# Cosine attention and a gated layer on one core: half products for h of chunk 2 and half of chunk 1, one order from chunk 0's last output tiles on, output stores on SyncE

## The chip, the cores and the metric

The kernel runs on 1 core of one Trainium2 chip. The metric is the device time of one execution in microseconds (us); less is better. A run of the kernel before gives 273.4 us as the median of 3 (273.35, 273.4, 274.11).

## The reference

Inputs q, k, v have the shape 8 batches x 8 heads x 576 rows x 64. w_in is 512 x 2048, w_out 2048 x 512, beta has 2048 entries. Everything is float32 in memory.

```python
theta = np.pi / 2.0 * pos / S
def phi(x, c, s):
    r = np.maximum(x, 0.0)
    return np.concatenate([r * c, r * s], axis=-1)
q_p = phi(q, cos_w, sin_w); k_p = phi(k, cos_w, sin_w)
kv  = np.einsum('bhsf,bhsd->bhfd', k_p, v); z = np.sum(k_p, axis=2)
num = np.einsum('bhsf,bhfd->bhsd', q_p, kv)
den = np.einsum('bhsf,bhf->bhs', q_p, z)[..., None] + 1e-06
x   = (num / den).transpose(0, 2, 1, 3).reshape(B * S, H * D)   # 4608 x 512
h   = x @ w_in
g   = h * (1.0 / (1.0 + np.exp(-beta * h)))
out = g @ w_out                                                # 4608 x 512
```

## The kernel before, in words

**Two halves in one stream.** The attention goes by batch b = 0 to 7, the layer by chunk c = 0 to 8 of 512 rows of x (TCH). A batch has nine blocks of 64 rows, a chunk eight, so chunk c needs the last c blocks of batch c−1 and the first 8−c of batch c. While the layer works on chunk c, the attention of batch b = c+1 is made beside it, and the raw inputs of later batches are loaded.

**Attention of one batch.** load_raw (L79) loads q, k and v of a batch by one DMA each, all issued on SyncE; there is one buffer for each of the three (raw_q, raw_k, raw_v), so the load of the next batch can start only when the last reader of the old one is done. q_relu and k_relu (L192 on ACT, L193 on DVE) take the positive part in bf16. v_scale (L217 on ACT, L219 on DVE) multiplies v by the cosine or the sine of its row; one instruction does one of nine blocks. kv_mm (L276) makes k_p^T v in PSUM and kv_take (L286) copies it out. q is transposed by one DMA, q_turn_dma (L259), on SyncE; the sine copy of it is a multiplication by tan (tan_mul, L223) on GpSimd or DVE. num_mm (L297) makes numerator and denominator, x_rden (L308, L312) the reciprocal, x_mul (L319) the quotient, and x_turn_dma (L367), again a DMA on SyncE, transposes it into xt, the chunk's input. For the first blocks of a run PE transposes instead (x_turn_pe, L356, with copies at L361 and L363).

**The layer's first product, two forms.** In the whole form (h_group) one 128-column tile of h is four matmuls of 128x512 (h_mm, L386) and one silu on ACT (h_act, L394). In the half form (h_pair) two column tiles together form a 2 by 2 block product over halves of the columns, of the depth and of the rows, done with seven products in place of eight by sums of operands (Strassen and Winograd); each product is two matmuls of 128x256 (L511). That needs four sums of w_in for each pair (wh_sum, L443, in the buffers wx["w"] and wx["v"]), four sums of x for each chunk (x_sum, L455), and in PSUM a seed copy (op "c", ACT, L480), a kept partial (op "d" ACT or "D" DVE, L484) and two additions (ops "e", "f", DVE, L487); the two silu are ops "A" and "B" (h_silu, L420). Before, chunks 0, 1 and 2 use the whole form and chunks 3 to 8 the half form.

**The second product.** Chunk 0 is whole (o_mm, L544). Chunk 1 (o_fast, L563) and chunks 2 to 8 (o_pair, L621) use the same seven products for four output tiles of 128 rows, with sums of g (g_sum, L406, into S1 to S4) and of w_out (T1 to T4, L876 to L879). Each output tile is copied to o_sb (in o_pair: A, B on ACT and X, Y on DVE, both L658/L661 as whole tiles; pieces P, Q on ACT and U, V on DVE, L652) and stored in two halves of rows (store, L537). The stores of chunks 0 to 6 are issued on GpSimd, those of chunk 7 on SyncE, those of chunk 8 on GpSimd, SyncE and ACT.

**What sets the order.** The tile framework is told to keep the program's order (manual_schedule), and each engine runs its instructions in that order. Up to chunk 1 the order is written as loops over slots: 32 slots of chunk 0 (slots 0 to 15 tiles of h, 16 to 23 and 24 to 31 the output), then 16 slots of h of chunk 1 with the attention's steps hung on some of them, then a list of o_fast's ops. Chunk 2 starts with 16 slots of whole h tiles (h_first). From chunk 2's output on, ORDERS holds a string of ops for each chunk, and chunk() runs them one after the other: "h25" is product 5 of h pair 2, "h2c5" its seed into bank 5, "ox6" product 6 of the first output pair, "s30" a sum of g, "W61" a sum of w_in, "t1" a sum of x, "K05"/"kT" kv products and copy, "N12" numerators into bank 2, "x1" the quotient and its transpose, "v3"/"w3" a v_scale of the sine on ACT / of the cosine on DVE, "k2" and "q1" relus, "g0" a multiplication on GpSimd, "TQ" the batch's q transpose, "Lq", "Lk", "Lv" a raw load. PSUM has eight banks, all named by hand; o_sb has four buffers, xt three, g five.

Of the kernel before, what the change touches and what calls it, by code (L numbers as in the profile page):

```python
# [16 lines left out]
P = 128  # L17
# [5 lines left out]
def kernel(  # L23
# [175 lines left out]
    def k_relu(b, j0=0, j1=4, eng="dve", n0=0, n1=NQ):  # L199
        relu(rk.rearrange("q n j d -> q j n d")[:, j0:j1, n0:n1], raw_tile(b, "k")[:, j0:j1, n0:n1], eng)  # L200
# [207 lines left out]
    def g_sums(c, i0, i1):  # L408
        for kind in (1, 3, 2, 4):
            got = g_sum(c, i0, i1, kind)  # L410
        return got
# [10 lines left out]
    def wx_tiles():  # L422

        wx["w"] = stage.tile([P, 4, 512], FP32, name="w_stage", tag="w_stage").rearrange("q a f -> q (a f)").bitcast(
            BF16).rearrange("q (k s g f) -> q k s g f", k=4, s=4, g=2)
        wx["v"] = stage.tile([P, 4, 512], FP32, name="w_stage", tag="w_stage").rearrange("q a f -> q (a f)").bitcast(
            BF16).rearrange("q (k s g f) -> q k s g f", k=4, s=4, g=2)
        wx["x"] = stage.tile([P, 4, 512], FP32, name="w_stage", tag="w_stage").rearrange("q a f -> q (a f)").bitcast(
            BF16).rearrange("q (s n c) -> q s n c", s=8, n=NB // 2)
        wx["q"] = stage.tile([P, 4, 512], FP32, name="w_stage", tag="w_stage").rearrange("q a f -> q (a f)").bitcast(  # L430
            BF16)[:, 0 : 2 * NQ * P].rearrange("q (s n c) -> q s n c", s=2, n=NQ)

    def w_sum(jt, i):
        return wx["w" if jt % 4 == 0 else "v"][:, jt // 4, i]

    def wh_sum(jt, kind):
        f0 = jt % 4
        A11, A12, A21, A22 = (win[jt // 4][:, 2 * jp : 2 * jp + 2, f * P : (f + 1) * P]
                              for f in (f0, f0 + 1) for jp in range(2))
        s1, s2, s3, s4 = (w_sum(jt, i) for i in range(4))  # L440
        o, l, r, op = {1: (s1, A21, A22, ALU.add), 2: (s2, s1, A11, ALU.subtract),
                       3: (s3, A11, A21, ALU.subtract), 4: (s4, A12, s2, ALU.subtract)}[kind]
        return nc.vector.tensor_tensor(o, l, r, op=op)  # L443

    def wh_sums(jt):
        for kind in (1, 3, 2, 4):
            got = wh_sum(jt, kind)
        return got
# [55 lines left out]
    def h_pair(c, i):  # L504
# [16 lines left out]
        s1, s2, s3, s4 = (w_sum(jt0, k_) for k_ in range(4))  # L521
# [10 lines left out]
    def store(c, tt, o_sb, m0=0, m1=DM, eng=None):  # L532
        for hf in range(2):
            bb, n = divmod((c * TCH + tt * P) // HP + hf, NQ)
            own = (nc.gpsimd if c < 7 or (c == NTC - 1 and tt == 0) else
                   (nc.sync, nc.scalar)[hf] if c == NTC - 1 and tt % 2 else nc.sync)
            (eng or own).dma_start(out=out_v[bb, n][:, m0:m1], in_=o_sb[hf * HP : (hf + 1) * HP, m0:m1])  # L537
# [225 lines left out]
    def rest():  # L763
# [16 lines left out]
        k_relu(1, 0, 2)  # L780
        q_relu(1, 0)
# [9 lines left out]
    def second():  # L791
# [22 lines left out]
        28: lambda: x_turn_pe(1, 0, 7, 4, ("act",), (0,)),  # L814
        29: lambda: x_turn_pe(1, 0, 7, 5, ("dve",), (1,)),
    }

    def num_rest():
        for n in range(7, NQ):
            for jp in range(2):  # L820
                num_mm(1, n, jp, 2, 2 * (n - 7) + jp)
        x_mul(x_rden(2, 0, 7, NQ, (0, 1)), 7, NQ)
        x_turn_dma(1, 7, NQ)

    def att_q(b, turn=True):
        q_relu(b, 0)
        q_relu(b, 1)
        if turn:
            q_turn_dma(b)
        if b + 1 < B and b != 3:  # L830
            load_raw(b + 1, "q")

    def v_half(b, cs, n0=0, n1=NQ, eng="dve"):
        if b >= B:
            return
        v_scale(b, cs, n0=n0, n1=n1, eng=eng)
        if cs == 1 and n1 == NQ and b + 1 < B:
            load_raw(b + 1, "v")

    def k_all(b):  # L840
        k_relu(b)
        if b + 1 < B:
            load_raw(b + 1, "k")

    def kv_all(b, bank=6, eng="dve"):
        kv_mm(b, 0, bank)
        kv_mm(b, 1, bank)
        kv_take((0, 1), bank, eng)
# [5 lines left out]
    for slot in range(32):  # L854
# [26 lines left out]
    wx_tiles()  # L881
    for slot in range(16):
        h_group(1, slot)
        if slot == 0:
            num_rest()
            att_q(2)
            v_half(2, 0)
        if 2 <= slot < 6:
            v_half(2, 1, slot + 3, slot + 4, "act")
        if slot == 4:  # L890
            k_all(2)
            v_half(2, 1, 0, 5)
        elif slot == 6:
            w_sums()
        elif slot == 10:
            kv_all(2, eng="act")
            for jp in range(2):
                tan_mul(nc.vector, qs_of(2)[:, jp], qts[0][:, jp], 0, NQ)
    q_relu(3, 0, "act")
    q_relu(3, 1, "act")  # L900
    q_turn_dma(3)

    def one_sums(kind):
        for i0 in range(0, JT // 2, 2):
            g_sum(1, i0, i0 + 2, kind)

    def ops(of, names):
        for n in names.split():
            of[n]()

    x, y = o_fast(1, 0, (2, 5, 4)), o_fast(1, 1, (3, 7, 6))
    ops(x, "1 c1")
    one_sums(1)
    ops(y, "1 c1")
    for t, bank in enumerate((4, 6, 0)):
        num_all(2, t, bank)
    one_sums(2)
    x_part(2, 0, 4)
    ops(x, "6 cu")
    ops(y, "6 cu")  # L920
    one_sums(3)
    ops(x, "2 5 c5")
    x_part(2, 1, 6)
    ops(x, "7")
    one_sums(4)
    ops(x, "a2 a7")
    ops(y, "7 2")
    got = wh_sums(0)
    x_part(2, 2, 0)
    load_raw(4, "q")  # L930
    q_tan(3, 0, got)
    q_tan(3, 1)
    ops(y, "a2 5 c5")
    ops(x, "3 a3 4 c4")
    ops(y, "a7 3 a3 4 c4")
    v_half(3, 0)

    ORDERS = {
# [153 lines left out]
```

## Time and profile before

| what | value |
|---|---|
| device time, median of 3 runs | 273.4 us (273.35 to 274.11) |
| span of the profiled execution | 272.7 us |
| time of the profiled execution beyond its span | not given; the median is 0.7 us above the span |
| granted clock of PE, 40 slices | 9 or more tenths in each |
| silu of half form (L420) / of whole form (L394) | 96 x 702 ns / 48 x 688 ns |
| additions of h (L487, first form) | 74 x 428 ns |
| seeds (L480) | 62 x 383 ns |
| sums of g (L406) | 66 x 418 ns |
| v_scale on ACT (L217) | 58 x 503 ns |
| output stores issued on GpSimd | 58, 33.9 us of issue |
| raw loads, median time from issue to landing | v 9.7, k 9.5, q 7.4 us |

How to read it: the profiler records every instruction of every engine. PE is the matmul engine, PEld its weight loads, DVE, ACT and POOL the vector, scalar and GpSimd engines, SP is SyncE, SPq its DMA issues. The busy share of an engine is the time in which it has at least one instruction running. Because instructions on one engine overlap at their ends, the mean duration of an instruction is more than the time between two of them in a stream; the latter is read from rows of the timeline, where a run of equal instructions has one start and one length.

### The profile page before, as it was taken

To read this page: it belongs to the slowest core of one execution; us is meant where nothing else is said; L and a number is where in the kernel's file an instruction comes from. 1 tells how busy PE (TensorE), PEld (TensorE's weight loads), DVE (VectorE), ACT (ScalarE), POOL (GpSimd) and SP (SyncE) were. 2 spreads that over 40 slices of the span, in tenths; PEclk is the share of its full clock that TensorE was granted. 3 is DMA by queue.
4 is the path that set the end of the run, shared out by engine and by line. 5 is a ranking of instruction groups with operands and counts; after the bars stand their busy time and mean duration, and the time that the engine had idled before them with its cause. 6 is when DMAs were issued, how large, how long until landed. Compare 5 with 4: busy or idle time off the path is not lost.

```text
span 272.7 us, 8970 instructions
## 1 busy us (share of the span) xinstructions
PE 265.3 (97%) x3712; PEld 206.8 (76%) x3712; DVE 224.0 (82%) x596; ACT 188.4 (69%) x384; POOL 68.3 (25%) x89
## 2 busy tenths in 40 slices
PE   8899999999899999999999999999999999999994
PEld 8554455455784588888888888888888888888883
DVE  5989969499989889789989997899589768757852
ACT  4778777796419656899489966996696179428920
POOL 1444000510078000660085009300840060000001
PEclk9999999999999999999999999999999999999999
DMA  6999999999969999994589439943600570015005
GB/s 237 374 395 383 392 390 319 379 201 336 284 130 311 240 348 226 240 313 103 147 216 370 92 58 223 332 71 62 181 2 2 61 185 1 2 27 130 0 2 155
DMA packets 50681, 54.00 MB, mean 198 GB/s; under 512 B 31232, under 2 KB 31760, under 8 KB 50640
## 3 DMA queue, kind: packets, MB, share of 16 engines
q1 hardware_dynamic: 47504, 45.55, 59.1%
q0 software_dynamic: 2784, 7.61, 9.6%
q8 instruction: 29, 0.48, 0.7%
q10 hardware_dynamic: 352, 0.27, 0.4%
q14 instruction: 12, 0.10, 0.1%
HBM read 36.71 MB, written 9.44 MB: 169 GB/s over the span
## 4 chain that ended last, share of the span: by engine, by line
PE 85%; DVE 9%; DMA 3%; SPq 1%; issue 1%; ACT 1%; DVEq 0%
PE ps L621 32%; PE ps L511 27%; PE ps L386 10%; PE ps L544 5%; PE ps L563 4%; PE ps L297 3%; DMA raw_v<-in_v_dram 3%; PE ps L276 3%; DVE vb L219 1%; DVE xs L319 1%; DVE qs L223 1%; SPq L79 1%; DVE S L406 1%; DVE rk L193 1%; DVE qb L193 0%
## 5 line engine op out<-in xcount | busy, mean ns | idle before, releaser
L537 POOL DMA_DIRECT2D out_dram<-o_sb x58 | 33.9, 591 | 147.3 <-ACT o_sb L658 86.3
L420 ACT ACTIVATE g_t<-ps,beta 128x512 bf16<-128x512 f32 x96 | 60.3, 702 | 1.4 <-PE ps L511 1.3
L621 PEld LDWEIGHTS <-S 128*128 128x128 bf16 x448 | 43.4, 98 | 5.2
L511 PE MATMUL ps<-w_stage 128*128 128x256 bf16 x288 | 46.6, 272 | 0.1
L386 PE MATMUL ps<-xt,win 128*128 128x512 bf16 (+1 forms) x196 | 42.8, 375 | 0.1
L511 PEld LDWEIGHTS <-w_stage 128*128 128x128 bf16 x384 | 37.3, 98 | 5.1 <-issue 0.2
L487 DVE TENSOR_TENSOR ps<-ps,p 128x256 f32<-128x256 f32 x74 | 30.5, 428 | 8.6 <-PE ps L511 3.0
L394 ACT ACTIVATE g_t<-ps,beta 128x512 bf16<-128x512 f32 x48 | 32.3, 688 | 7.2 <-PE ps L386 7.1
L621 PEld LDWEIGHTS <-g_t 128*128 128x128 bf16 x336 | 32.3, 98 | 4.5 <-ACT g_t L420 0.4
L386 PEld LDWEIGHTS <-win 128*128 128x128 bf16 x196 | 18.7, 98 | 21.1 <-issue 0.5
L511 PE MATMUL ps<-xt,win 128*128 128x256 bf16 x192 | 32.9, 273 | 0.0
L511 PEld LDWEIGHTS <-win 128*128 128x128 bf16 x288 | 28.0, 98 | 3.4
L621 PE MATMUL ps<-wout,g_t 128*128 128x256 bf16 x224 | 28.9, 273 | 0.0
L406 DVE TENSOR_TENSOR S<-g_t 128x512 bf16<-128x512 bf16 (+1 forms) x66 | 25.7, 418 | 3.3 <-ACT g_t L420 1.7
L480 ACT COPY ps<-ps 128x256 f32<-128x256 f32 x62 | 22.6, 383 | 7.5 <-PE ps L621 4.0
L217 ACT ACTIVATE vb<-raw_v,sin 128x256 bf16<-128x256 f32 (+1 forms) x58 | 26.0, 503 | 1.5 <-DMA raw_v<-in_v_dram 1.5
L621 PE MATMUL ps<-T,S 128*128 128x256 bf16 x224 | 26.6, 273 | 0.0
L621 PE MATMUL ps<-wout,S 128*128 128x256 bf16 x224 | 26.4, 273 | 0.0
L319 DVE TENSOR_TENSOR xs<-ps,rden 128x768 bf16<-128x768 f32 (+4 forms) x26 | 22.8, 884 | 0.9 <-DVE rden L312 0.2
L223 POOL TENSOR_TENSOR qs<-qt,tanr 128x1152 bf16<-128x1152 bf16 x6 | 14.3, 2387 | 27.4 <-PE ps L563 21.0
L658 ACT COPY o_sb<-ps 128x512 f32<-128x512 f32 x11 | 6.3, 587 | 20.1 <-PE ps L621 20.1
L487 DVE TENSOR_TENSOR ps<-ps,u 128x256 f32<-128x256 f32 x36 | 15.3, 427 | 5.3 <-PE ps L511 3.3
(112 smaller groups left out, 414.7 us busy)
## 6 DMA issues: line engine op xcount, KB each, us to landing
raw_v<-in_v_dram SPq DMA_DIRECT2D x7, 1152.0 KB, 9.7
raw_k<-in_k_dram SPq DMA_DIRECT2D x7, 1152.0 KB, 9.5
raw_q<-in_q_dram SPq DMA_DIRECT2D x7, 1152.0 KB, 7.4
out_dram<-o_sb POOLq DMA_DIRECT2D x58, 128.0 KB, 4.5
w_stage<-in_moe_w_in_dram SPq DMA_DIRECT2D x3, 1024.0 KB, 12.8
w_stage<-in_moe_w_out_dram SPq DMA_DIRECT2D x2, 1024.0 KB, 7.9
w_stage<-in_moe_w_out_dram SPq DMA_DIRECT2D x4, 512.0 KB, 11.9
out_dram<-o_sb SPq DMA_DIRECT2D x10, 128.0 KB, 2.4
```

Source lines behind the costliest of these rows:

```text
L217: got = nc.scalar.activation(o, a, AF.Copy, scale=t[:, n : n + 1])
L223: return eng.tensor_tensor(dst.rearrange("q n (g p) -> q n g p", g=2), src.rearrange("q n (g p) -> q n g p", g=2), tanr[:, n0:n1].unsqueez ...
L319: nc.vector.tensor_tensor(o.rearrange("q j n s d -> q j (n s) d"), nv[:, :, a:z, :, 0:D].rearrange("q j n s d -> q j (n s) d"), rden[:, :, ...
L386: nc.tensor.matmul(ps[:, h_bank(c, jt), i * 64 : (i + w) * 64], lhsT=win[jt // 4][:, mi, (jt % 4) * P : (jt % 4 + 1) * P], rhs=xt[:, i : i ...
L394: return nc.scalar.activation(gs[c, jt // 4][:, jt % 4], ps[:, h_bank(c, jt)], AF.Silu, scale=beta[:, jt : jt + 1])
L406: return nc.vector.tensor_tensor(o, l, r, op=op)
L420: return nc.scalar.activation(gs[c, jt // 4][:, jt % 4], bank, AF.Silu, scale=beta[:, jt : jt + 1])
L480: return nc.scalar.copy(at("a", 0), at("b", 0))
L487: nc.vector.tensor_tensor(dst, at("b", 0), st["p5"], op=ALU.add)
L511: nc.tensor.matmul(dst, lhsT=l[:, g], rhs=r[:, :, g * HP : (g + 1) * HP], start=start and g == 0, stop=g == 1, skip_group_check=True)
L537: (eng or own).dma_start(out=out_v[bb, n][:, m0:m1], in_=o_sb[hf * HP : (hf + 1) * HP, m0:m1])
L621: nc.tensor.matmul(dst, lhsT=l(i), rhs=r[:, i], start=start and i == 0, stop=i == order[-1], skip_group_check=True)
```

## The change

- **h of chunk 2 and of pairs 4 to 7 of chunk 1** goes to the half form. Chunk 1's first eight tiles (0 to 7) stay whole (ops "G0" to "G7").
- **Sums of w_in** are made a slice (512 columns) at a time, both pairs of it together: 16 instructions of 128x512 in place of 32 of 128x256. Six of them stand in rest(), which runs in chunk 0, the others in the new orders.
- **One order.** The slot loop ends at slot 26. The rest of chunk 0 (its last output tiles as ops "Sb" to "Sf", the last transposes on PE as "R0", "R1"), chunk 1 and all of chunk 2 become strings in ORDERS. An op may name another chunk ("1/ox6") or another batch ("r0@2"), so ops of one chunk stand among those of the next. The strings of chunks 3 to 8 are new as well: the last output ops and some sums of a chunk stand among the h ops of the next.
- **New ops**: k_relu on DVE ("l", "kk"), q_relu on ACT ("r"), a v_scale of the cosine on ACT ("z") or of the sine on DVE ("u"), the sums of w_out one by one ("M1" to "M4").
- **Stores** of chunks 0 to 7 are issued on SyncE, and of chunk 8 the first tile's on GpSimd and the others' as before.
- **Order on SyncE** around chunk 1: before, q, v, k of batch 2, a transpose of x, the q transpose of batch 2, q, k, v of batch 3, the q transpose of batch 3. After: q, v, k of batch 2, q of batch 3, the q transpose of batch 2, eight stores of chunk 0, a transpose of x, v of batch 3, k of batch 3, a transpose of x, q of batch 4.
- **The last output ops** of chunk 8: before "oyU oyf ox4 oxY oy4 oy3 oyB oyV", after "oy3 ox3 oxf oyf oxX ox4 oy4 oyU oyV oxY oyY".

The core of the diff:

```diff
-    def w_sum(jt, i):
-        return wx["w" if jt % 4 == 0 else "v"][:, jt // 4, i]
-    def wh_sum(jt, kind):
-        f0 = jt % 4
-        A11, A12, A21, A22 = (win[jt // 4][:, 2 * jp : 2 * jp + 2, f * P : (f + 1) * P]
-                              for f in (f0, f0 + 1) for jp in range(2))
+    def w_sum(sl, i):
+        return wx["wv"[sl // 2]][:, sl % 2, i]
+    def wh_sum(sl, kind):
+        A11, A12, A21, A22 = (
+            win[sl][:, 2 * jp : 2 * jp + 2].rearrange("q g (u r f) -> q g u r f", u=2, r=2)[:, :, :, r]
+            for r in range(2) for jp in range(2))
...
-        s1, s2, s3, s4 = (w_sum(jt0, k_) for k_ in range(4))
+        s1, s2, s3, s4 = (w_sum(jt0 // 4, k_)[:, :, jt0 % 4 // 2] for k_ in range(4))
...
-            own = (nc.gpsimd if c < 7 or (c == NTC - 1 and tt == 0) else
-                   (nc.sync, nc.scalar)[hf] if c == NTC - 1 and tt % 2 else nc.sync)
+            own = (nc.sync if c < NTC - 1 else nc.gpsimd if tt == 0 else (nc.sync, nc.scalar)[hf] if tt % 2 else nc.sync)
...
         k_relu(1, 0, 2)
+        wx_tiles("wv")
+        for sl, kind in ((0, 1), (0, 3), (0, 2), (0, 4), (1, 1), (1, 3)):
+            wh_sum(sl, kind)
         q_relu(1, 0)
...
-    for slot in range(32):
+    for slot in range(27):
...
+        0: (
+            "Sb R0 Sc Sd 1/M1 W21 t1 Se W31 W22 1/r1@2"),
+        1: (
+            "h417 r0@2 0/R1 0/W33 Lq@3 h45 TQ@2 0/Sf M4 G6 G7 u8@2 0/t2 h4d h4c2 u5@2 u6@2 Z0 G0 v2@2 G3 h514 h5c3 h616 "
...
+            "h72 h5f s11 h6f h76 h7e h5A kk@2 h43 Lv@3 h4B y0 h63 h54 h5B h6A h4A h64 h73 h77 G1 h7f G2 h7A y1 Lk@3 K02 "
+            "K1 h74 kT s10 h6B oy17 M2 N03 N25 h7B oyc0 x0 s20 r1@3 s13 s12 r0@3 s32 s33 v2 z3 ox12 oy2 N13 s40 oy5 ox5 "
+            "s22 s21 s23 v7 oy6 z0 v8 oxc1 oxd z7 Lq@4 z4 x1 ox2 s30 oyd z2 v3 u4 oye"),
...
+        elif k_ in "vwuz":
+            got = v_scale(batch(1), "wzvu".index(k_) // 2, n0=n, n1=n + 1, eng="act" if k_ in "vz" else "dve")
...
+    wx_tiles("xq")
+    held = None
+    for c in range(NTC):
         for op in ORDERS[c].split():
...
+            other, slash, rest_ = op.partition("/")
+            held = do(int(other), rest_, held) if slash else do(c, op, held)
```

More of the change, by code (lines that the diff above doesn't have):

```diff
@@ L420, in h_silu, with wx_tiles @@
         return nc.scalar.activation(gs[c, jt // 4][:, jt % 4], bank, AF.Silu, scale=beta[:, jt : jt + 1])
[L422 to L431, printed above, removed]
[L433 to L440 removed]
+    def wx_tiles(names):
+        for name in names:
+            t = stage.tile([P, 4, 512], FP32, name="w_stage", tag="w_stage").rearrange("q a f -> q (a f)").bitcast(BF16)
+            if name in "wv":
+                wx[name] = t.rearrange("q (k s g u f) -> q k s g u f", k=2, s=4, g=2, u=2)
+            elif name == "x":
+                wx[name] = t.rearrange("q (s n c) -> q s n c", s=8, n=NB // 2)
+            else:
+                wx[name] = t[:, 0 : 2 * NQ * P].rearrange("q (s n c) -> q s n c", s=2, n=NQ)
+    def w_sum(sl, i):
[4 more added lines that the diff above has]
+            for r in range(2) for jp in range(2))
+        s1, s2, s3, s4 = (w_sum(sl, i) for i in range(4))
         o, l, r, op = {1: (s1, A21, A22, ALU.add), 2: (s2, s1, A11, ALU.subtract),
@@ L899 @@
[L899 to L919, printed above, removed]
@@ L1058, with w_out_sum, pair @@
-    h_first(2)
-    held = None
-    for c in range(2, NTC):
-        held = chunk(c, held)
+    def w_out_sum(kind):
+        z = ALU.subtract
+        o, l, r = {1: (T1, B12, B11), 2: (T2, B22, T1), 3: (T4, B21, T2), 4: (T3, B22, B12)}[kind]
+        return nc.vector.tensor_tensor(o, l, r, op=z)
+    ORDERS = {
[70 rows of a table added]
+    }
+    pairs, parts = {}, {}
+    def pair(c, name):
+        if (c, name) not in pairs:
+            n = "xy".find(name[1])
+            pairs[c, name] = (h_pair(c, int(name[1])) if name[0] == "h" else o_pair(c, n) if name[0] == "o" else
+                              o_fast(c, n, ((2, 5, 4), (3, 7, 6))[n]))
+        return pairs[c, name]
```

196 lines of the change are left out of this document (64 added, 132 removed), and 100 rows, old and new, of the table ORDERS.

## The prediction

> **What bounds the kernel now.** I read the busy times first, then the chain of work that ended last, then the order in time of each engine.
>
> ```profile
> span 272.7 us, 8970 instructions
> PE 265.3 (97%) x3712; PEld 206.8 (76%) x3712; DVE 224.0 (82%) x596; ACT 188.4 (69%) x384; POOL 68.3 (25%) x89
> ...
> PE 85%; DVE 9%; DMA 3%; SPq 1%; issue 1%; ACT 1%; DVEq 0%
> ```
>
> PE is busy 97% of the span and carries 85% of the chain, and the granted clock is at its top in all forty slices. So time falls only if PE gets less to do or stops less. In the timeline of PE, from 18.65 us to its last end at 269.02, one idle stretch is longer than 0.25 us: 0.96 us ahead of chunk 1's output products.
>
> ```profile
> 51.70 8.81 PE L386 MATMUL ps<-xt,win 128*128 128x512 bf16 x40
> 61.59 4.49 PE L386 MATMUL ps<-xt,win 128*128 128x512 bf16 x20
> 70.15 1.91 PE L563 MATMUL ps<-T,S 128*128 128x256 bf16 x16 [0.96 <-ACT p L602]
> 104.31 1.04 PE L621 MATMUL ps<-wout,g_t 128*128 128x256 bf16 x8
> 105.18 1.91 PE L621 MATMUL ps<-wout,S 128*128 128x256 bf16 x16
> ```
>
> Columns: start, length, engine, line, operation, shape, count. These rows give what a matmul costs in a stream, which isn't the mean duration of the group table (375 and 273 ns there, because matmuls overlap). Twenty more of 128x512 take 8.81 − 4.49 us: **0.216 us each**. Eight more of 128x256 take 1.91 − 1.04: **0.109 us each**.
>
> **The products (fewer, smaller matmuls).** Twelve pairs of h tiles (eight in chunk 2, four in chunk 1) leave the whole form, 2 tiles x 4 matmuls of 128x512 = 8 per pair, for seven products of two 128x256 = 14 per pair. 96 x 0.216 = 20.7 us go, 168 x 0.109 = 18.3 us come: **−2.4 us** of PE. [...]
>
> **The work around the products.** Each half-product pair brings a seed (ACT, L480), a keep, two adds (DVE, L487) and two silu; each sum of w_in and of x is made once. Counted from the two orders, adds go 124 to 152, seeds 62 to 76, x sums 24 to 32, and the 32 small w_in sums become 16 of twice the width. With their mean durations this is about +8 us on DVE and +16 on ACT over the whole kernel. Neither can bound it on average (224 and 188 of 272), but locally it can: from the rest of batch 1's numerators to chunk 2's kv products I count, at the pace that these engines keep back to back (length less 0.08 us on DVE, less 0.11 on ACT), 24.5 us of DVE (62 instructions) and 24.1 of ACT (52) beside 25.2 of PE, and in the first 11 us DVE has 12.1 to PE's 11.0. The later stages, whose orders before are as full, lose about 0.1 us in 10. I take **+0.3 us**; the bounds are 0 and 62 x 0.08 = 5.0 us, the latter if no two DVE instructions overlapped their ends, which the rows of before (1.42 us for four of 0.416) exclude. The range takes +1.1, DVE's excess over those 11 us. The six w_in sums in chunk 0 (not shown by the trace in this shape; between 0.28, the small form, and 0.42, the x sum of the same size) are 6 x 0.34 = 2.0 us, in 2.25 us that DVE idles there from 36.9 us, waiting for raw_q: nothing. With that cover gone it would be 2.0 on DVE, still ahead of PE's need. Moving stores off GpSimd saves nothing by itself: its 58 issues (33.9 us) delay only GpSimd's own multiplications, which nothing here waits for.
>
> **The stall at 69 us.** The chain in order of time ends its DVE stretch with sums for chunk 1's output:
>
> ```profile
> 66.66 2.02 DVE S L406 x6
> 68.69 1.15 ACT qb L192
> 69.83 0.27 ACT p L602
> 70.15 4.86 PE ps L563 x43
> ```
>
> ACT's q relu of batch 3 stands in front of the copy that PE waits for. In the new order half of chunk 1's h work lies between those sums and their readers, and the relus stand after them; this stall goes: **−1.0 us** (bounds 0, if DVE is late there again, and −1.0). Late next are batch 3's v rows, below.
>
> **SyncE.** Batch transposes and raw loads are issued there, in order:
>
> ```profile
> 61.46 0.39 SPq L79 DMA_DIRECT2D raw_v<-in_v_dram  x1
> ...
> 69.86 3.51 SPq L259 DMA_TRANSPOSE qt<-qb  x1
> ...
> 110.12 1.50 SPq L79 DMA_DIRECT2D raw_q<-in_q_dram  x1
> 111.73 11.25 SPq L259 DMA_TRANSPOSE qt<-qb  x1
> ...
> 139.62 0.46 SPq L79 DMA_DIRECT2D raw_q<-in_q_dram  x1
> 140.18 10.77 SPq L259 DMA_TRANSPOSE qt<-qb  x1
> ...
> 266.31 3.82 SPq L537 DMA_DIRECT2D out_dram<-o_sb  x6
> ```
>
> A transpose of q holds the queue 3.5 to 11.3 us. Each time the hold ends when the loads issued ahead of it have landed: that raw_q lands 12.8 us after its issue, at 122.92, and the hold ends at 122.98; the next lands at 150.97, the hold ends at 150.95. The change puts q of batch 3 in front of batch 2's transpose, and behind that the eight stores of chunk 0 (0.636 us each, 3.82 / 6), a transpose of x and only then v and k of batch 3. Walking the queue: v and k of batch 2 land at 52.3 and 55.2 us, as before (40.83 + 11.5, 41.43 + 13.8); q of batch 3, issued at about 50, lands 2.9 behind them (their spacing), at 58.2; until then the transpose holds SyncE. Stores to 63.3, the x transpose (1.25) to 64.6, v of batch 3 issued at 64.7. Alone in flight such a load lands 6.4 us later (rows from 5.6 to 7.3): 71.2. ACT gets to its first v scale of batch 3 at about 69.1 by the count of the order; it then waits 2.1 us, with five scales (0.40 each) and the seed of chunk 1's first output pair (0.38) behind it, on which PE's next product depends: 71.2 + 5 x 0.40 + 0.38 = 73.6 to 73.7, where PE comes at 72.3: 1.4 us. A transpose of x, queued behind k of batch 3 (74.1), lands at 74.85 (0.7 after the load ahead of it, as at 104.0 and 104.75), 0.3 us late. Sum **+1.7 us**; bounds 0 (no hold: v lands at 67.7) and 2.6 (the slowest of those landings). No later transfer is late by the same walk.
>
> **The end.** Now PE ends at 269.02, DVE copies 0.42 us, the last store is issued at 269.58 and lands 2.19 later, and the span ends 0.9 behind that: 3.65 behind PE. In the new last order DVE takes both the halves of one output tile and, as whole 128x512 copies, the last two: U, V, X of the other, Y. Five stores then stand in SyncE's queue behind PE's end, 0.55 to 0.64 us each, where one did; the last is issued 1.7 us behind PE's end in place of 0.56: **+1.2 us** (bounds 0, if they don't queue, and 1.4).
>
> **Sum.** −2.4 − 1.0 + 1.7 + 0.3 + 1.2 = −0.2: a span of 272.5. The median of the runs shown is 273.4, 0.7 above the profiled span; the profiled execution is taken as equal to the median. So the forecast is **273.1 us**: little change, because the queue and the end give back what the products save. Its own range is 272.3 to 274.2. A measurement tells 0.3%, 0.8 us, from no change.
>
> **Rivals.**
> 1. *The hold is covered.* If q of batch 3 lands early or ACT is late anyway at its v scales, 1.7 us go: **271.4**. For it: at 55.47 us the same transpose held only 4.65 us; against: two holds of 11 us that ended exactly with a load. Chance 0.27. [...]
> 2. *The hold repeats, and it is slower.* SyncE now has, in each chunk, eight stores (5.1 us), three loads (1.5), four x transposes (5.0) and one hold of 3.5 to 11.5: 15 to 23 of about 27 us. If in one more chunk a raw load is issued less than 6.4 us ahead of its first reader, another 1.7 us come, and with DVE's 0.1 to 0.2 behind it **274.9**. It decides from that point on, and each further chunk adds as much. Chance 0.25.
> 3. *Neither wait nor tail.* Stores overlap at the end and v is in time: 273.4 − 2.4 − 1.0 + 0.3 = 270.3, **270.2** with the order's rounding. Chance 0.08.
>
> The forecast has 0.40. Its low and high reach 270.8 and 275.3: rival 1 and 2 with their spreads, the far tail of 2 and most of 3 left out. Faster by over 0.3% (below 272.6): rivals 1 and 3 and a little of the forecast, 0.40. Within: most of the forecast, 0.35. Slower (above 274.2): rival 2, 0.25.
>
> **What would show it.** The products: PE's busy time near 263, and 92 matmuls at L386 of 128x512. The stall: no gap at chunk 1's first output product. SyncE: a transpose that starts near 50.7 us and lasts 7 us, raw_v of batch 3 issued near 64.7 and landing near 71; an idle stretch of ACT by raw_v at L217, and PE gaps of 1.4 and 0.3 us between 72 and 75 us. The end: last store issued 1.7 us behind the last matmul. Wrong would be: no such hold, PE waiting for DVE in chunks 1 and 2 for more than a microsecond, or ACT waiting for raw_v in later chunks.

## The result and the profile after

The changed kernel takes 282.3 us (median of three executions, 282.23 to 284.23) against 273.75 (273.35 to 274.53) of the kernel before: **3.4% slower**, ratio 1.0337, 95% interval 1.0296 to 1.0378. The forecast was 273.1, its range 270.8 to 275.3. One execution each of the changed kernel, pool_stores, combo and combo2 was over 1.5% slower than the fastest of its kernel, at a mean granted clock of 0.986, 0.984, 0.563 and 0.754, and is left out of the times; the traces of combo and combo2 are of these executions and are not read here. The profiled execution of the changed kernel took 282.34 us, with a span of 280.3 us.

A second profile of the kernel before (the run before_again below) has a span of 271.4 us and a time of 273.2, so 1.8 lie around the span, about as after (2.0). The profile that the prediction was made from had the longer span, 272.7. I compare with the second one from here on.

From the page of the changed kernel, the busy time of PE, DMA's instruction queue (count, MB, share), and the chain:

```profile
PE 264.9 (95%) x3784; PEld 213.9 (76%) x3784; DVE 232.1 (83%) x606; ACT 201.5 (72%) x411; POOL 35.6 (13%) x33
...
q8 instruction: 29, 0.48, 0.7%
...
PE 67%; DMA 17%; DVE 10%; issue 2%; ACT 1%; SPq 1%; POOL 0%; POOLq 0%; ACTq 0%; DVEq 0%
```

PE's share of the chain fell from 85 to 67%; DMA has 17 where it had 3. PE's busy time is nearly what it was (265.3 us before), so the new time is stops of PE, not work. These are the rows of PE's timeline from 18 us on before which it had been idle, with what ended the wait (those under 0.3 us are left out, but for the third):

```profile
59.23 0.38 PE L502 MATMUL ps<-w_stage 128*128 128x256 bf16 x2 [0.38 <-DVE ps L478]
68.30 0.92 PE L611 MATMUL ps<-wout,g_t 128*128 128x256 bf16 x7 [0.52 <-issue]
73.42 1.03 PE L611 MATMUL ps<-wout,g_t 128*128 128x256 bf16 x8 [0.20 <-ACT ps L471]
76.13 0.38 PE L502 MATMUL ps<-xt,win 128*128 128x256 bf16 x2 [1.67 <-DMA xt<-xs]
132.38 0.42 PE L276 MATMUL ps<-vb,rk 64*64 64x130 bf16 x15 [1.08 <-issue]
159.78 1.10 PE L276 MATMUL ps<-vb,rk 64*64 64x130 bf16 x64 [0.72 <-issue]
183.95 0.22 PE L297 MATMUL ps<-kv,qt 64*64 64x65 bf16 x4 [0.38 <-issue]
219.38 0.60 PE L502 MATMUL ps<-w_stage 128*128 128x256 bf16 x4 [1.45 <-DVE w_stage L446]
```

The idle time in brackets is less than what a stop costs, since the modelled end of a matmul lies behind the start of the next (a 128x256 matmul is 0.273 us long at a spacing of 0.109). For the ledger I take from the trace, for each two matmuls in order, the time from start to start less the normal spacing of that shape (0.109, 0.216 us and so on), and call a stop what is above 0.2 us. The table's first row then holds the counts of matmuls at their normal spacing, which is the same in both kernels.

| us, from 18 us on | before (second profile) | after | difference |
|---|---|---|---|
| PE's end without stops and small gaps | 265.89 | 263.49 | −2.40 |
| stops with nothing waited for ("issue"), at 67.5, 131.1, 158.8, 183.4 | 0 | 3.44 | +3.44 |
| stops for a transpose of x, at 74.2 and 217.7 | 0 | 3.44 | +3.44 |
| stop for ACT behind raw_v, at 73.0 | 0 | 0.36 | +0.36 |
| other stops, mostly for DVE and ACT | 0.70 | 2.06 | +1.36 |
| small gaps | 1.17 | 1.69 | +0.52 |
| from PE's end to the end of the span | 3.65 | 5.79 | +2.14 |
| span | 271.41 | 280.27 | +8.86 |

So the products gave what they should, and everything else took. Of the 2.06 us of other stops, 0.23 stands at 18.3 us in both kernels, 0.54 at 58.6 us, and six of 0.20 to 0.39 us between 120 and 207 us.

### The profile page after: what moved, and what is told of

Read it like the earlier page. It is cut to its first block, busy times and chain, and to the rows that moved or that the text cites. A ratio compares the mean times of both kernels' runs of the same rounds, so it can differ in the third digit from the quotient of the medians.

```text
span 280.3 us, 9175 instructions
## 1 busy us (share of the span) xinstructions
PE 264.9 (95%) x3784; PEld 213.9 (76%) x3784; DVE 232.1 (83%) x606; ACT 201.5 (72%) x411; POOL 35.6 (13%) x33
## 4 chain that ended last, share of the span: by engine, by line
PE 67%; DMA 17%; DVE 10%; issue 2%; ACT 1%; SPq 1%; POOL 0%; POOLq 0%; ACTq 0%; DVEq 0%
PE ps L611 30%; PE ps L502 29%; DMA raw_v<-in_v_dram 7%; DMA raw_q<-in_q_dram 5%; DMA xt<-xs 4%; PE ps L276 2%; PE ps L386 2%; PE ps L297 2%; DVE xs L319 2%; DVE vb L219 1%; DVE ps L478 1%; SPq L79 1%; DVE S L406 1%; ACT g_t L416 1%; ACT ps L471 1%
## 5 line engine op out<-in xcount | busy, mean ns | idle before, releaser
L502 PE MATMUL ps<-w_stage 128*128 128x256 bf16 x360 | 60.9, 272 | 2.0 <-DVE w_stage L446 1.4
L502 PEld LDWEIGHTS <-w_stage 128*128 128x128 bf16 x480 | 46.7, 98 | 10.0 <-issue 3.4
L611 PEld LDWEIGHTS <-S 128*128 128x128 bf16 x512 | 49.7, 98 | 6.0
L478 DVE TENSOR_TENSOR ps<-ps,p 128x256 f32<-128x256 f32 x91 | 37.8, 428 | 10.3 <-PE ps L611 4.6
L502 PE MATMUL ps<-xt,win 128*128 128x256 bf16 x240 | 43.1, 272 | 1.7 <-DMA xt<-xs 1.7
L406 DVE TENSOR_TENSOR S<-g_t 128x512 bf16<-128x512 bf16 x64 | 25.5, 416 | 1.6 <-ACT g_t L416 1.5
L502 PE MATMUL ps<-xt,w_stage 128*128 128x256 bf16 x120 | 22.6, 272 | 0.2 <-DVE ps L478 0.2
L386 PE MATMUL ps<-xt,win 128*128 128x512 bf16 (+1 forms) x100 | 22.1, 371 | 0.1
L502 PE MATMUL ps<-w_stage,win 128*128 128x256 bf16 x120 | 21.2, 273 | 0.0
L217 ACT ACTIVATE vb<-raw_v,sin 128x256 bf16<-128x256 f32 (+1 forms) x37 | 17.2, 502 | 2.4 <-DMA raw_v<-in_v_dram 2.4
```

The lines of the kernel that those rows point to most:

```text
L217: got = nc.scalar.activation(o, a, AF.Copy, scale=t[:, n : n + 1])
L386: nc.tensor.matmul(ps[:, h_bank(c, jt), i * 64 : (i + w) * 64], lhsT=win[jt // 4][:, mi, (jt % 4) * P : (jt % 4 + 1) * P], rhs=xt[:, i : i ...
L478: nc.vector.tensor_tensor(dst, at("b", 0), st["p5"], op=ALU.add)
L502: nc.tensor.matmul(dst, lhsT=l[:, g], rhs=r[:, :, g * HP : (g + 1) * HP], start=start and g == 0, stop=g == 1, skip_group_check=True)
L611: nc.tensor.matmul(dst, lhsT=l(i), rhs=r[:, i], start=start and i == 0, stop=i == order[-1], skip_group_check=True)
```

## The experiments

All are edits of the changed kernel, except where the kernel before is named. Times are medians, ratios go against the kernel before on the same chip. The interval of the changed kernel overlaps those of all its edits but pool_stores, which is slower, and combo3, which is faster; what the other edits do is read from their traces, each of one execution.

| run | us | ratio, 95% interval |
|---|---|---|
| before_again | 273.2 | one execution |
| before_stores | 273.84 | 1.0015 (0.9997 to 1.0033) |
| before_dense | 277.81 | 1.0159 (1.0121 to 1.0197) |
| changed kernel | 282.3 | 1.0337 (1.0296 to 1.0378) |
| phase | 285.23 | 1.0428 (1.0361 to 1.0494) |
| tail | 283.31 | 1.0350 (1.0314 to 1.0387) |
| lq_behind | 285.33 | 1.0445 (1.0376 to 1.0513) |
| pool_stores | 285.84 | 1.0445 (1.0422 to 1.0468) |
| x0_first | 283.36 | 1.0350 (1.0300 to 1.0400) |
| combo | 282.01 | 1.0302 (1.0264 to 1.0341) |
| spread | 284.03 | 1.0367 (1.0334 to 1.0400) |
| combo2 | 281.86 | 1.0304 (1.0272 to 1.0335) |
| spread2 | 283.22 | 1.0371 (1.0328 to 1.0415) |
| combo3 | 280.08 | 1.0236 (1.0214 to 1.0258) |

### The stops without a named wait: phase, before_dense

The four stops lie at PE's 1973rd, 4019th, 4785th and 5552nd matmul or weight load: steps of 2046, 766 and 767; with the 2, 2 and 1 other instructions of PE that the trace has between them these are 8, 3 and 3 times 256. The page counts 29 fetches on the instruction queue, 0.48 MB, so 16 KB each; PE has 7,568 matmuls and weight loads, 29.6 times 256. In the trace, a fetch starts 2.49, 2.48, 2.52 and 2.36 us ahead of PE's going on. Rival: PE waits for data in a way that the profile doesn't name. To tell them apart, phase shifts the program by 48 PE instructions. (By the count of matmuls and weight loads, the fetch started 206, 203, 130 and 178 ahead of the four stops, not 204 to 224 as the expectation has it.)

```diff
-    warm_pe(58, 48)
+    warm_pe(34, 82)
```

> The changed kernel with 34 warm-up matmuls of 82 columns at the very start in place of 58 of 48: the same columns, but 24 matmuls and 24 weight loads fewer on PE ahead of everything. Theory A (PE waits for its own instructions): in the changed kernel PE stops at 67.5, 131.1, 158.8 and 183.4 us for 0.52 to 1.08 us with nothing that it waits for, each time 204 to 224 instructions behind the start of a 16 KB fetch of the instruction queue and at the same place modulo 256 instructions, in or right behind a run of short attention matmuls. With 48 instructions fewer the places move out of these runs: the four stops go, about 3.2 us in all, and the time falls from 282.3 to about 279. Rival B (PE waits there for something of its data that the profile does not name): the four stops stay where they are and the time stays at 282.3 within 0.5.

```profile
48.18 0.22 PE L297 MATMUL ps<-kv,qs 64*64 64x65 bf16 x3 [0.71 <-issue]
...
134.96 0.22 PE L297 MATMUL ps<-kv,qt 64*64 64x65 bf16 x3 [0.58 <-issue]
140.06 1.65 PE L611 MATMUL ps<-T,S 128*128 128x256 bf16 x7 [2.39 <-issue]
...
167.60 0.76 PE L276 MATMUL ps<-vb,rk 64*64 64x130 bf16 x40 [0.33 <-issue]
```

These are PE's rows of phase. The stops are at counts 1203, 3759, 4015 and 4781: the last two where they were (4019 and 4785; the trace of phase lacks four matmul records, 3756 of 3760), but now in front of **other** instructions, the one at 4015 in the middle of an output product's eight matmuls, which wait for nothing there; and 3759 is 256 ahead of 4015. Data does not stay at a count when the program moves under it by 48. Theory A holds for the cause. Its size did not come: the moved places met other short groups, and in the profiled execution, the slowest of the four, the clock was halved for 3.4 us behind the stop of 2.4 us and twice more (below). The time rose.

In the kernel before, where no such stop is, I made one group of numerators four times:

```diff
-... ox12 h74 h4B N15 h7B N03 ...
+... ox12 h74 h4B N15 N15 N15 N15 h7B N03 ...
```

> The kernel before, in which chunk 5 makes one group of numerators (48 matmuls of 64x65, 0.51 us on PE) four times in a row in place of once, into the same bank; the output is the same, and the work three times repeated is 144 matmuls with 144 weight loads, 288 PE instructions. Theory A (PE's instructions come in blocks of 256, each fetch takes 2.4 us or more from its start to the first instruction, and short matmuls use a block up in 1.4 us): besides 1.5 us of work, PE stops at one or two block boundaries in or behind the repeated groups, 1 to 3 us each, without waiting for anything that the profile names: 273.7 to 277 to 279. Rival B (the stops in the changed kernel have another cause): plus 1.5 us of work at most, 275.2, and no unnamed stop.

```profile
180.45 0.19 PE L297 MATMUL ps<-kv,qt 64*64 64x65 bf16 x1
182.92 0.22 PE L297 MATMUL ps<-kv,qt 64*64 64x65 bf16 x3 [2.27 <-issue]
```

One stop, in the middle of the repeated groups, at count 5551, where the changed kernel has one at 5552. The time rose by 4.3 us in the median. In the profiled execution (279.13 us, 5.6 more) 1.5 is work and 2.5 the stop, and the clock was halved for 3.4 us behind it. Shown by this run: PE stopped (2.27 us idle) where it used up 256 instructions, here 128 short matmuls and their weight loads, faster than the next 16 KB came. In the changed kernel kv products (72 matmuls in 1.15 us) and groups of numerators (48 in 0.51), or two such groups, stand close together at the end of chunks 1, 3, 4 and 5. Before, kv products stand alone; the one long row, three groups of numerators at 67.4 us, got by: its fetch started at 66.0 us, 1.4 us ahead of the row. With the fetch ahead of the first stop counted as that of the block which begins there, and so on fetch by fetch, the last three of the changed kernel (233.23, 247.18 and 261.69 us), late where the transfer engines have little to do (0 to 6 tenths busy in the page's last ten slices), start when PE is 264, 267 and 259 instructions short of their block, so about as it begins the one before.

### The queue of SyncE: lq_behind, pool_stores, before_stores

The changed kernel's SyncE, in order of time:

```profile
50.29 0.37 SPq L79 DMA_DIRECT2D raw_q<-in_q_dram  x1
50.76 7.77 SPq L259 DMA_TRANSPOSE qt<-qb  x1
58.62 5.04 SPq L527 DMA_DIRECT2D out_dram<-o_sb  x8
63.74 1.25 SPq L367 DMA_TRANSPOSE xt<-xs  x1
65.10 0.52 SPq L79 DMA_DIRECT2D raw_v<-in_v_dram  x1
65.72 1.74 SPq L79 DMA_DIRECT2D raw_k<-in_k_dram  x1
68.72 1.26 SPq L367 DMA_TRANSPOSE xt<-xs  x1
...
88.57 1.03 SPq L79 DMA_DIRECT2D raw_q<-in_q_dram  x1
89.69 7.26 SPq L259 DMA_TRANSPOSE qt<-qb  x1
```

The hold is there, 7.77 us, and ends with the load ahead of it (landed 58.61); v was issued at 65.10 and landed at 70.97, k at 75.28, the transpose of x behind it at 75.99, and PE went on at 76.13. The last two rows show a later hold, which ends at 96.96 us as its raw_q lands (96.95). Then the load at 50.29 was put behind the transpose:

```diff
-... 0/W33 Lq@3 h45 TQ@2 0/Sf ...
+... 0/W33 h45 TQ@2 Lq@3 0/Sf ...
```

> The changed kernel with the load of batch 3's q issued behind batch 2's q transpose instead of ahead of it. Theory A (the prediction's queue): the transpose at 50.8 us then holds SyncE for 4.7 us (until k of batch 2 has landed, 55.4) in place of 7.8, everything behind it is issued 3 us earlier, v and k of batch 3 land 2 to 3 us earlier, and PE's stop of 1.67 us at 74.2 us, which ends with a transpose of x that lands 0.7 us behind that k, falls under 0.3: 282.3 to about 280.5. Rival B: the transpose is held by something else than the load ahead of it, lasts 7 us or more again, and nothing moves: 282.3. Rival C: q of batch 3 now shares the transfer engines with k and v of batch 3, these land no earlier than before, and the stop stays above 1 us: about 282.

```profile
50.20 5.20 SPq L259 DMA_TRANSPOSE qt<-qb  x1
55.50 0.53 SPq L79 DMA_DIRECT2D raw_q<-in_q_dram  x1
56.12 6.25 SPq L527 DMA_DIRECT2D out_dram<-o_sb  x8
62.47 1.25 SPq L367 DMA_TRANSPOSE xt<-xs  x1
63.82 0.53 SPq L79 DMA_DIRECT2D raw_v<-in_v_dram  x1
64.45 0.46 SPq L79 DMA_DIRECT2D raw_k<-in_k_dram  x1
68.61 1.25 SPq L367 DMA_TRANSPOSE xt<-xs  x1
```
```profile
69.61 3.00 PE L611 MATMUL ps<-wout,g_t 128*128 128x256 bf16 x14 [1.93 <-issue]
77.22 0.38 PE L502 MATMUL ps<-xt,win 128*128 128x256 bf16 x2 [0.24 <-DMA xt<-xs]
```

(SyncE's rows, then PE's.) The hold fell to 5.20 us and ended as k of batch 2 landed (55.4): the first link of theory A is shown. The next links are not. v was issued 1.3 us earlier, but landed at 70.91, where it had landed at 70.97; k landed at 74.87 (75.28), and the transpose of x that PE waits for at 77.09, which is 1.1 us later than in the changed kernel. PE's stop there fell from 1.67 to 0.24 us because PE itself came about 2.5 us later. At the block boundary its instructions were late: the fetch started at 67.27 at count 1964, where in the changed kernel it started at 65.81 at count 1767, the stop of 0.52 became 1.93, and the clock was halved behind it. So the landings are as rival C has them, but not for its reason, since q of batch 3 had landed (61.89) before v was issued. Why v and k took longer is open. That the raw loads in flight delay the fetch is only argued; it fits pool_stores below too, where v and k were issued at 63.41 and 63.97 and the fetch started at 68.66.

```diff
-            own = (nc.sync if c < NTC - 1 else nc.gpsimd if tt == 0 else ...)
+            own = (nc.gpsimd if c < 7 or (c == NTC - 1 and tt == 0) else ...)
```

> The changed kernel with the stores of chunks 0 to 6 issued on GpSimd again, as in the kernel before. Theory A (the stores fill SyncE's queue): behind the hold at 50.8 to 58.5 us the transpose of x is issued at once and v of batch 3 at about 60 to 62 in place of 65.1, its k soon after, and PE's stop at 74.2 us (1.67) goes; the other stops (DVE and ACT in chunks 1 to 3, PE's four without a named cause, 1.45 at 217.7 for a transpose of x) stay: about 280.5. Rival B: raw_v and raw_k wait for their buffers' last readers, not for the queue, and are issued at the same times: 282.3. Rival C: GpSimd's multiplications come late behind the stores and PE waits for the sine copy of q: over 282.5.

Rival C, and more than it said. The stop at 74 us went: v was issued at 63.41 (theory A said 60 to 62), the transpose of x landed at 74.80, 1.2 us earlier, and PE came 2.3 us later. But the q transpose now held SyncE 10.76 us and landed at 64.98, so that DVE's sine copy came late (PE idle 1.19 us at 66.8), the stop at the block boundary behind it grew from 0.52 to 1.69, and at 113.9 PE stood 1.58 us. At that last place, GpSimd's multiplication, late behind four stores, met a sum on DVE:

```profile
111.58 2.64 DVE L446 TENSOR_TENSOR w_stage<-xt,w_stage 128x512 bf16<-128x512 bf16 x1
```
```profile
109.38 2.12 POOL L528 DMA_DIRECT2D out_dram<-o_sb  x4 [13.06 <-ACT o_sb L649]
111.52 2.40 POOL L223 TENSOR_TENSOR w_stage<-qt,tanr 128x1152 bf16<-128x1152 bf16 x1
```

(DVE's row, then GpSimd's.) A sum that takes 0.42 us elsewhere took 2.64 and ended 0.3 us behind GpSimd's multiplication. The other part alone, the kernel before with its stores on SyncE:

> The kernel before with one part of the change alone: the output stores of chunks 0 to 6 issued on SyncE in place of GpSimd. Theory A: the stores stand behind the q transposes that hold SyncE for 4 to 11 us, and raw loads and transposes of x behind the stores; PE or ACT then wait for them in some chunks: plus 1 to 4 us, 274.7 to 277.7. Rival B: the old orders issue stores and transposes at different times in a chunk, SyncE has the room, and nothing on the path moves: 273.7 within 0.5.

Rival B: 273.84 us, within 0.3% of the kernel before. In the old order the stores' place costs nothing; in the new order, putting them back on GpSimd costs more than it saves.

### The transpose for chunk 7: x0_first

At 217.7 us DVE's sum waits 1.75 us for a transpose of x of the first third of batch 7, which the order makes behind the second third.

```diff
-... h7f N14 x1 s21 ... N01 s22 ... s40 x0 s41 ...
+... h7f N04 x0 s21 ... N11 s22 ... s40 x1 s41 ...
```

> The changed kernel in which the first third of batch 7's numerators and quotients (blocks 0 to 2), one block of which chunk 7 needs, is made ahead of the second third, which only chunk 8 needs. Theory A: PE's stop at 217.7 us (1.45 idle, behind the first sum of x of chunk 7, which waits 1.75 us for a transpose of x issued at 214.5 and landed at 218.9) goes, since this transpose is issued about 3 us earlier: the stop is under 0.2 and the time falls by about 1.5, from 282.3 to 280.8. Rival B: PE stops at that place for its instructions (a 16 KB fetch started at 216.4, 3.0 us ahead of the stop's end): the stop stays above 1 us at the same count of PE instructions.

PE's rows from 214 to 222 us have no stop left: theory A. The time did not fall. In the profiled execution (283.54 us) the stop at 73.9 us was longer (2.90 us by the ledger's measure, where it was 1.83; k landed at 76.09 in place of 75.28), the clock was halved behind it, and the four stops at block boundaries were 0.8 us longer together. In this table (busy time in each stretch, the column after POOL is the granted clock) the second row is the one to see:

```profile
73.90:76.20 2.30, 0.28 (x3) 0.00 (x1) 1.43 (x4) 2.30 (x7) 0.00 (x0) 0.99 1.02 64
76.20:79.60 3.40, 2.68 (x13) 1.90 (x14) 0.35 (x2) 3.18 (x7) 0.00 (x0) 0.50 1.07 366
79.60:83.00 3.40, 3.40 (x33) 2.94 (x30) 3.33 (x9) 0.00 (x0) 0.00 (x0) 1.00 1.09 225
```

### The end: tail

The last rows of the changed kernel on PE, then DVE, then SyncE:

```profile
272.57 1.91 PE L611 MATMUL ps<-T,g_t 128*128 128x256 bf16 x16
```
```profile
273.38 0.75 DVE L642 COPY o_sb<-ps 128x256 f32<-128x256 f32 x2
274.04 0.90 DVE L651 COPY o_sb<-ps 128x256 f32<-128x256 f32 x2
```
```profile
271.81 5.56 SPq L527 DMA_DIRECT2D out_dram<-o_sb  x6
```

SyncE issues until 277.37, 2.9 us behind PE's end at 274.48.

```diff
-... oye oxe oy7 s43 ox7 oy3 ox3 oxf oyf oxX ox4 oy4 oyU oyV oxY oyY
+... oye oxe s43 ox7 oxf ox3 oxA oy7 oyU oyf ox4 oxY oy4 oy3 oyB oyV
```

> The changed kernel with the last output ops of chunk 8 in about the order of the kernel before: the last output tile by halves on DVE early, the other copies on ACT, one store behind the last matmul. Theory A: the stores that stand in SyncE's queue behind PE's end cost 2.1 us: the span ends 3.6 to 3.8 us behind the last matmul in place of 5.8, the time falls to about 280.2. Rival B: the products' order there matters too and PE stops for the sums of g, so that half or more of it is lost: 281.2 or more.

The span ended 3.9 us behind PE (276.53 to 280.43): theory A in size, 1.9 us. PE's end came 2.05 later, in part by the new order itself (a stop of 0.69 at 270.3 us, which waits for an addition on DVE), in part by other stops of that execution. So the end's cost is shown in the trace, not in the time.

### Do the costs add up: combo, spread, combo2, spread2, combo3

combo has lq_behind, x0_first and tail together.

> The changed kernel with three of the edits together: q of batch 3 loaded behind batch 2's transpose, the first third of batch 7 first, and the last output ops as before. Theory A (the stops are independent of each other): the span ends 3.9 us behind the last matmul in place of 5.8 (1.9), the stop at 217.7 us goes (1.5), the one at 74.2 stays small (1.4) but the one at 67.5, at an instruction block's boundary, grows as in the run with the load behind (minus 1.4): 282.3 to about 279. Rival B: what is taken away in one place comes back as a later stop of PE for ACT or DVE: over 281.

282.01 us, theory B's side. Then the short groups were moved apart. In spread and combo2 two kv products are made behind a v scale of the next batch and use that batch's rows, so these two do not compute the reference and their waits are not those of the changed kernel:

> The changed kernel in which the groups of short matmuls are moved apart at four places, nothing added or taken away: the last numerators of batch 2 behind two products of chunk 1's output, batch 5's kv products behind two output products of chunk 3, batch 6's kv products behind one of chunk 4, the last numerators of chunk 5 behind one output product. The 256 PE instructions ahead of each block boundary then take 4 us or more in place of about 2.5. Theory A (PE's instruction supply): the stops at the boundaries (0.68, 1.28, 0.92, 0.56 us at 67.5, 131.1, 158.8, 183.4) fall to under 0.3 each, the time by 2.5 to 3.4: about 279.5. Rival B (short matmuls move the stops to the next boundary, or the later copies of kv make PE wait for data): less than half of it is gained, 281 or more.

> All four edits on the changed kernel: the short groups apart, q of batch 3 behind the transpose, the first third of batch 7 first, the last output ops as before. Theory A (the stops are separate costs and add up): minus 3 (blocks), 1.5 (the stop at 217.7), 1.9 (the end) and 1.8 (74.2 and 72.9; the fetch that came late behind the loads no longer stops PE): 282.3 to about 274, as fast as the kernel before within 0.5. Rival B: what is left of the stops for DVE and ACT in chunks 1 to 4 (2.4 us) grows where PE now comes earlier: 276 or more.

284.03 and 281.86 us, far from both first theories; in spread's profile PE stands 4.15 us at 72 us behind ACT, which waits 4.43 for v of batch 3. spread2 and combo3 have the right order:

```diff
-... M2 N03 N25 h7B ... x1 ox2 s30 oyd ...              (chunk 1)
+... M2 N03 h7B ... x1 ox2 N25 s30 oyd ...
-... r0 4/K05 4/K1 s42 oye 4/kT s33 oy7 x2 t1 4/z0 ox6 oxd ...   (chunk 3)
+... r0 s42 oye s33 oy7 x2 t1 ox6 4/K05 4/K1 4/z0 oxd 4/kT ...
-... N21 5/K05 oxc7 5/K1 s23 s22 x2 oxd s40 5/u0 5/kT oy6 t1 ...  (chunk 4)
+... N21 oxc7 s23 s22 x2 oxd s40 oy6 5/K05 5/K1 5/u0 5/kT t1 ...
-... N03 N25 h7B s21 s40 s22 h6B s13 oy11 x0 ...         (chunk 5)
+... N03 h7B s21 s40 s22 h6B s13 oy11 N25 x0 ...
```

> The changed kernel with the groups of short matmuls moved apart as in the run before, but with each kv product still ahead of the v scales of the next batch, so that everything is computed as in the changed kernel. Theory A (PE's instruction supply): the stops at the block boundaries (0.68, 1.28, 0.92, 0.56 us) fall to 0.3 or less each; stops for data of up to 0.4 may come where kv is now copied later; no other stop changes: the time falls by 2 to 3 us, to about 280, as long as no stop reaches the length behind which the clock was halved in five of the runs (2.1 us and more). Rival B: the late kv copies make PE wait as long as the instructions did: 282 or more.

> The changed kernel with all four edits (short groups apart, q of batch 3 behind the transpose, the first third of batch 7 first, the last output ops as before), everything computed as in the changed kernel. Theory A (separate costs): minus 2.5 (blocks), 1.5 (the stop at 217.7), 1.9 (the end) and 1.5 to 1.8 (the stops at 72.9 and 74.2): 282.3 to about 274.5 to 275. Rival B: half of it comes back as stops for DVE, ACT or loads where PE now comes earlier: 278.

Rival B both times. In spread2 the stops at boundaries fell from 3.44 to 0.3 us, but all stops together are 9.08 us where they were 9.30: at 131.9 PE now stands 0.98 us for an addition on DVE, at 136.0 0.75 for the copy of kv, at 72.2 1.17 for ACT, and the stop for a transpose of x at 74.8 grew from 1.83 to 2.36 us. The stop at 217.7 went, though nothing was edited there. The new stops stand where short groups were taken away, so it seems that these had filled the waits and the fetch had run in them; no run shows that apart. combo3 is 280.08 us: of the 7.4 us or more expected of its four edits, 2.3 came. There too v of batch 3 was issued earlier (64.34) and landed no earlier (71.28). Its PE rows show where the rest went:

```profile
59.49 0.38 PE L502 MATMUL ps<-w_stage 128*128 128x256 bf16 x2 [0.54 <-DVE ps L478]
70.10 0.22 PE L297 MATMUL ps<-kv,qt 64*64 64x65 bf16 x2 [0.54 <-issue]
73.73 1.03 PE L611 MATMUL ps<-wout,g_t 128*128 128x256 bf16 x8 [0.58 <-ACT ps L471]
85.87 0.38 PE L502 MATMUL ps<-xt,win 128*128 128x256 bf16 x2 [0.88 <-ACT ps L471]
```

What fills the stretch is seen in the busy times from 50 to 78 us (length, then PE, PEld, DVE, ACT, POOL), of the second profile of before, then of the changed kernel, then of combo3:

```profile
50.00:78.00 28.00, 27.96 (x413) 18.53 (x412) 26.02 (x60) 18.42 (x34) 6.56 (x9) 1.00 1.01 273
```
```profile
50.00:78.00 28.00, 25.24 (x410) 17.99 (x409) 24.93 (x62) 26.48 (x57) 0.00 (x0) 1.00 1.04 284
```
```profile
50.00:78.00 28.00, 26.33 (x418) 18.92 (x416) 25.89 (x65) 26.39 (x57) 0.00 (x0) 1.00 1.12 297
```

Before, PE was full and ACT had 9.6 us to spare. Now ACT has 1.5 and DVE 3, and the rows show PE waiting for DVE and for ACT in turn. Which order of ACT's and DVE's work would let PE through is left open; no version that ran beats the kernel before.

### The profile that the prediction used: before_again

> The kernel before, unchanged, for a second profile. Theory A: the stop of 0.96 us at 69 us, which the prediction took off as a gain, belongs to the one execution that was profiled (the two variants of the kernel before that ran have 0.2 there), so the span is about 271.7 with a stop of 0.2. Rival B: it is there in every execution of this kernel: 0.9 or more.

Theory A: span 271.4, and the output products at L563 follow without a gap that the profile lists; by the ledger's measure the stop is 0.22 us where it was 1.14.

## Why the prediction was wrong

**The step that failed** is that the sum has no term for PE's own instructions. "The products" and "The work around the products" price PE's stream by its spacing and ask only whether DVE and ACT keep pace; that PE's instructions are there in time is put at nothing, without a reason. In its place the runs showed 3.44 us of stops at the ends of blocks of 256 instructions, the largest part of the 9.2 us between forecast and result. Nothing in the profile of before shows such a stop, but its queue of 29 fetches (0.48 MB on its page, as after) and the counts of the short matmuls were there to be set against each other. The rest is in the other terms: a stall that was no gain (1.0 us), a later transpose put at nothing (1.61), too little for the work around the products (1.6), for the end (0.9) and for SyncE (0.5); with the 3.44 these make 9.1.

- **The work around the products**, +0.3: 1.88 in the ledger, 1.36 of stops for DVE and ACT and 0.52 of small gaps. The totals were not far off (DVE 8.1 us more for 8, ACT 13.1 more for 16), and ACT is full where the prediction looked (26.5 of 28 us). It asked whether DVE and ACT keep pace over a stretch; that they do does not mean that PE never waits inside it (0.54 us at 58.6). Most of these stops stand outside, between 120 and 207 us, where it took 0.1 us in 10. That engines which are all full lose wherever they cross is argued from these places; no run isolates it.
- **Products**, −2.4: right, since the spacing is 0.109 and 0.216 us in the changed kernel too; with the counts that gives the ledger's −2.40. PE's busy time, the sign named for it, fell only to 264.9 in place of 263: a matmul's modelled length (0.27 us) is longer than its spacing, so each stop hides up to 0.16 us in it.
- **The stall at 69 us**, −1.0: wrong. It belonged to the one execution that was profiled. "The profiled execution is taken as equal to the median" was the mistake: a span 1.3 us longer than that of a second execution. This alone put the forecast 1 us too low.
- **SyncE**, +1.7: 2.19 measured, near by luck. The walk to v was right (issued 65.10 against 64.7, landed 70.97 against 71.2; ACT waited 1.45 us against 2.1), but the two parts came out the other way round. The wait of ACT was to cost PE 1.4 us and cost 0.36, because PE, stopped at 58.6 and 67.5, came 0.8 us later than walked; the transpose of x was to cost 0.3 and cost 1.83, because k and the transpose behind it landed 1.1 us later than walked. And a shorter hold did not bring v any earlier (lq_behind), so that the hold costs what the walk says is not shown. Nor does each hold end with a load: of six in the kernel before, four end within 0.1 us of the landing of the load ahead (73.33, 122.93, 150.97, 177.86 us) and two 0.6 and 4.9 us behind it; of six in the changed kernel, two within 0.1 us (58.61, 96.95) and two 0.6 and 0.9 us behind it, and at 140.82 and 169.64, with the loads ahead landed, the transpose still took 2.82 us. "No later transfer is late by the same walk" was wrong by 1.61 at 217.7 us: the walk followed SyncE's queue, but that transpose was late because its quotient was made late.
- **The end**, +1.2: right in kind, 2.14 in size. The last issue began 1.9 us behind PE's end (1.7 forecast), but took 1.0 and landed 3.0 behind its start in place of 2.2, with twelve stores from three engines in the last 8.5 us.
- **Rival 1** (the hold is covered) is refuted as to the hold (7.77 us) and ACT's wait (1.45), though that wait cost PE only 0.36. **Rival 2** (the hold repeats, and a reader waits) came in its first half: the hold of 7.26 us at 89.69 ended with a load again, but from 72 us on neither ACT nor DVE waited more than 0.31 us for a raw load. In combo3 ACT waits 1.31 us at 83.6 for a q transpose. **Rival 3** (neither wait nor tail) is refuted by both.

## What to carry to other kernels

Where a change takes work from the bound engine and gives it to two that are nearly full, look at who waits for whom, stretch by stretch, not at the averages; and check that one profiled execution has the median's time before a stop in it is counted as a gain. Count PE's instructions as a resource of its own: several groups of very short matmuls in a row can run it dry (four groups of 48 in before_dense: a stop of 2.27 us). A cost shown by a trace is not yet a gain when taken away: it may be filling another wait. And when a stop shrinks after an edit, see whether the thing waited for came earlier or the one who waits came later.

## What the runs showed of the hardware

- PE's instructions came in blocks of 256: two stops of phase lie 256 matmuls and weight loads apart (3759 and 4015), the four of the changed kernel 2048, 768 and 768 instructions. At 26 of the 28 stops of 0.3 us or more at a block's boundary, in the traces read here, 2.2 to 2.9 us passed from the start of a fetch to PE's going on, whatever stood there; at the other two (phase, pool_stores) 4.2 and 3.8, and there the fetch itself took 2.8 and 2.3 us in place of about 1 (0.96 to 1.24 at the changed kernel's four).
- After a stop of PE the granted clock was 0.5 for 3.41 us (twice that once): after stops of 2.10 (lq_behind), 2.46 (before_dense), 2.56 (phase), 2.90 (x0_first) and 4.31 us (spread), and once around two stops of 1.32 and 1.62 us (phase, 78.4 us). It was not after 1.83 (the changed kernel), 2.10 (tail) and 2.35 (spread2). Behind the stop in lq_behind 14 matmuls of 128x256 took 3.00 us, where in pool_stores the same 14 took 1.69. By half of the 3.41 us, an estimate, it costs about 1.7 us each time where PE has work. That the times of these edits vary by up to 4 us between executions (lq_behind 283.65 to 287.64, phase 283.78 to 287.71) may come from it; only one execution of each was traced.
- A DVE sum of 0.42 us took 2.64 beside a GpSimd multiplication of 2.40 us (pool_stores). It is not alone: in the kept traces 27 of the 59 DVE instructions that touch no PSUM and began beside such a multiplication took over a fifth longer than elsewhere (another one, a v_scale of 0.35 us, took 2.06 in before_stores, and one at 144.03 us 0.78 in the changed kernel), and each of the 27 ended 0.15 to 0.29 us behind the multiplication. The 570 that read or write PSUM and began beside one kept their length.
